# Attention output through folded weights, a hand-set order, and weight sums made early, in a linear-attention and token-mixer kernel

## The chip, the cores and the metric

One core of one Trainium2 chip. The metric is device time in microseconds (us), median over runs. A profiled execution has a span that is about 1.8 us shorter than the time of the same run; spans and moments within them come from the profile, medians from the timed runs. TensorE (PE) multiplies, VectorE (DVE) and ScalarE (ACT) do the elementwise work, SyncE (SP) issues nearly all DMAs, GpSimd (POOL) is nearly idle. PSUM is the memory in which matmuls add up their results. The granted clock is the share of TensorE's full clock that the chip let it have.

## The reference, cut to what matters

Batch 1, 2048 tokens, width 1024, 32 heads of 32, mixer width 3584, all bfloat16.

```python
pq, pk = phi(q), phi(k)                        # phi(t) = (t+1 if t>0 else exp(t)) + 1e-6
kv  = einsum("bhsd,bhse->bhde", pk, v)         # per head 32x32
z   = einsum("bhsd->bhd", pk)
num = einsum("bhqd,bhde->bhqe", pq, kv)
den = einsum("bhqd,bhd->bhq", pq, z)[..., None] + 1e-6
h   = x + (num / den).reshape(B, S, D) @ wo
# then a mixer over tokens: two layer norms of h, u = gelu(hn^T w1 + b1), y = u w2 + b2, h + y^T
```

## The kernel before: the parts that the change touches

The stages are: keys and values; the **Q phase** (query projection, with numerators and denominators of earlier tokens between its units); the **output projection** (16 tiles of 128 tokens, each "seeded": its residual tile is copied into PSUM, and the matmuls add to it); the **first mixer** (7 quads, each of two groups of 256 of the 3584 columns); the second mixer. The products of both mixers use 7 block products where plain ones need 8; a quad further does two of its seven products (p1 and p5) together, again by 7 in place of 8 ("inner").

```python
def attn_num_den(i):                       # per tile of 128 tokens
    for j in range(ND):                    # 8 matmuls, 128 numerator + 4 denominator columns
        nc.tensor.matmul(nd_ps[...], lhsT=pqT[:, j, i*P:(i+1)*P], rhs=ndrhs[:, j, :], start=True, stop=True)
    ... # ACT: ln, exp(-x) of 36 columns; DVE: 3 multiplies out of PSUM into o_sb
def attn_transpose(i, o_sb):
    nc.sync.dma_start_transpose(out=pqT[:, :, i*P:(i+1)*P], in_=o_sb[:])

def out_proj(i):
    xr = xrs.pop(i)                        # residual tile, loaded three tiles ahead
    h_bf = a3w.tile([P, D], BF16, name="h_bf")      # pool a3w: 3 buffers
    for dc in range(NDC):
        ap_ = acc_tile()                            # 5 PSUM banks in a ring
        nc.scalar.copy(ap_, xr[...])                # seed
        ... # 8 matmuls: pqT x wo
        nc.scalar.copy(h_bf[...], ap_)
        nc.vector.bn_stats(st[:, dc, :], ap_)
    ... # bn_aggr, scale, and:
    nc.sync.dma_start(h_dram[i][:], h_bf[:])
# ... after it: normalize_h(i - 2), which reads h_bf; at odd i also four differences ("combine")

# the first mixer's start: two products in a row, without the inner form
nxt = Mixer1(1)
pend = run_pair(cur, [], nxt)              # Mixer1(0)
cur, nxt = nxt, quad1(1)
pend = run_pair(cur, pend, nxt, after1=sums1, after5=sums5)
```

## Time and profile before

573.12 us median of 3 runs (573.01 to 573.24), span 571.5 us.

Part 4 of the page, the chain that ended last, by engine:

```profile
PE 95%; DVE 3%; ACT 1%; issue 1%; DMA 1%; ACTq 0%
```

The window sums by stage: the stretch, its length, then busy time (and instructions) of PE, PE's weight loads, DVE, ACT and POOL, the granted clock, DMA share and GB/s. The rows are the Q phase, the output projection, the first mixer, the rest.

```profile
core 0: us, PE busy (x) PEld busy (x) DVE busy (x) ACT busy (x) POOL busy (x), PEclk, DMA share, GB/s
125.92:178.14 52.22, 52.22 (x315) 26.68 (x313) 35.89 (x95) 34.69 (x79) 0.00 (x0) 1.00 0.66 167
178.14:235.50 57.36, 57.36 (x291) 26.73 (x289) 50.04 (x114) 40.12 (x100) 0.00 (x0) 1.00 0.56 149
235.50:403.03 167.53, 166.47 (x929) 90.64 (x929) 91.60 (x182) 79.34 (x163) 0.00 (x0) 1.00 0.25 76
403.03:571.50 168.47, 165.25 (x925) 89.87 (x923) 118.76 (x146) 34.14 (x73) 0.00 (x0) 1.00 0.47 127
```

PE is busy for the whole of the two attention stages; the others have slack. A busy PE may still run below its rate, so I read the rate from the starts of matmuls. PE's timeline in the Q phase (start, length, engine, line, operation, tiles, shape, count):

```profile
134.55 0.63 PE L1118 MATMUL nd_ps<-ndrhs,pqT 128*128 128x132 bf16 x8
135.02 3.61 PE L1019 MATMUL acc_t<-xnT,wq_sb 128*128 128x512 bf16 x16
138.47 0.63 PE L1118 MATMUL nd_ps<-ndrhs,pqT 128*128 128x132 bf16 x8
```

From 134.55 to 138.47 is 3.92 us. Sixteen matmuls of 512 columns take 138.47 - 135.02 = 3.45 us, 0.216 us each, and the 8 numerator ones 0.47 us. That is the exchange rate for the rest of the text. At the turn into the mixer PE does wait (the brackets give the idle time before a row and what ended it):

```profile
235.50 1.68 PE L297 MATMUL psA<-hE,wq 128*128 128x512 f16 x7
237.34 0.38 PE L297 MATMUL psA<-hE,wq 128*128 128x512 f16 x1 [0.15 <-DVE hE L1189]
237.55 1.67 PE L297 MATMUL psE<-hE,sa 128*128 128x512 f16 x7
239.96 1.02 PE L297 MATMUL psA<-hO,wq 128*128 128x512 f16 x4 [0.74 <-ACT psB L316]
```

### The profile page before, as it was taken

The page shows a single profiled execution, that of the slowest core. Times are in us where ns is not written, and L with a number is a line of the kernel's source. Part 1 is how long each engine was busy: PE and PEld are TensorE (multiplying, and loading weights), DVE is VectorE, ACT ScalarE, POOL GpSimd, SP SyncE. Part 2 cuts the span into 40 slices and gives each one's busy share as a digit, 9 for nine tenths or more (in the row PEclk, how much of TensorE's full clock was granted, in tenths as well). Part 3 has the DMA queues.
Part 4 walks back from the last instruction along what each step waited for, and adds up shares of the span by engine and source line. Part 5 has one row for each costly group of instructions (what it writes and reads, how often), then busy time and mean ns, then how long its engine had stood idle before and what let it go on. Part 6 is the DMA issues. An engine that isn't in the chain of part 4 may idle for free.

```text
span 571.5 us, 8308 instructions
## 1 busy us (share of the span) xinstructions
PE 563.7 (99%) x3124; PEld 293.3 (51%) x3124; DVE 390.2 (68%) x759; ACT 272.0 (48%) x585; POOL 1.8 (0%) x8
## 2 busy tenths in 40 slices
PE   7999999999999999999999999999999999999997
PEld 3444444455554444346555565555445655645643
DVE  6898887546767879873735627453979749659625
ACT  4747777666667776445445354453220411311211
POOL 1000000000000000000000000000000000000000
PEclk9999999999999999999999999999999999999999
DMA  9933432029536753104041340413892932912111
GB/s 303 357 76 79 89 74 38 19 96 323 118 72 127 177 178 111 55 2 147 1 148 28 120 148 1 148 48 81 205 255 84 244 96 75 278 56 73 38 47 46
DMA packets 97800, 66.61 MB, mean 117 GB/s; under 512 B 32082, under 2 KB 91744, under 8 KB 97760
## 3 DMA queue, kind: packets, MB, share of 16 engines
q1 hardware_dynamic: 97024, 65.42, 41.7%
q10 hardware_dynamic: 672, 0.66, 0.3%
q8 instruction: 24, 0.39, 0.3%
q14 instruction: 16, 0.13, 0.1%
q0 software_dynamic: 64, 0.01, 0.0%
HBM read 50.34 MB, written 8.39 MB: 103 GB/s over the span
## 4 chain that ended last, share of the span: by engine, by line
PE 95%; DVE 3%; ACT 1%; issue 1%; DMA 1%; ACTq 0%
PE psB L297 10%; PE psC L297 10%; PE acc_t L1019 9%; PE acc_t L1167 9%; PE psC L208 7%; PE psA L297 7%; PE psI L230 7%; PE psB L208 6%; PE psI L208 6%; PE psB L750 4%; PE psC L750 4%; PE psA L750 4%; PE psA L208 3%; PE acc_t L674 2%; PE psE L750 2%; PE psE L297 1%
## 5 line engine op out<-in xcount | busy, mean ns | idle before, releaser
L297 PEld LDWEIGHTS <-sa 128*128 128x128 f16 x436 | 42.6, 98 | 46.8 <-issue 0.7
L1019 PE MATMUL acc_t<-xnT,wq_sb 128*128 128x512 bf16 x256 | 58.0, 379 | 0.0
L1167 PE MATMUL acc_t<-wo_sb,pqT 128*128 128x512 bf16 x256 | 56.1, 379 | 0.0
L208 PEld LDWEIGHTS <-wq 128*128 128x128 bf16 (+1 forms) x357 | 34.5, 98 | 31.3
L297 PEld LDWEIGHTS <-wq 128*128 128x128 bf16 (+1 forms) x324 | 31.6, 98 | 33.1 <-issue 1.0
L208 PE MATMUL psC<-gs,wq 128*128 128x512 f16 (+2 forms) x210 | 45.0, 365 | 0.0
L1167 PEld LDWEIGHTS <-pqT 128*128 128x128 bf16 x256 | 24.8, 98 | 29.0
L1019 PEld LDWEIGHTS <-wq_sb 128*128 128x128 bf16 x256 | 24.5, 98 | 27.4
L166 ACT ACTIVATE e_sb<-acc_t 128x512 bf16<-128x512 f32 x40 | 23.9, 597 | 26.5 <-PE acc_t L1019 24.3
L170 DVE TENSOR_SCALAR e_sb<-e_sb 128x512 bf16<-128x512 bf16 x64 | 18.5, 289 | 25.4 <-ACT e_sb L166 24.8
L208 PEld LDWEIGHTS <-sa 128*128 128x128 f16 x231 | 22.6, 98 | 18.6
L750 PEld LDWEIGHTS <-xs 128*128 128x128 f16 x208 | 20.0, 98 | 23.3 <-DVE xs L736 1.3
L208 DVE TENSOR_TENSOR ot<-ot,hr 128x512 bf16<-128x512 bf16 (+2 forms) x27 | 11.2, 415 | 28.1 <-ACT ot L406 27.7
L333 ACT COPY psC<-psB 128x512 f32<-128x512 f32 x22 | 12.5, 570 | 35.1 <-PE psB L297 21.5
L297 PE MATMUL psB<-hT,sa 128*128 128x512 f16 x112 | 28.4, 379 | 0.0
L441 DVE TENSOR_TENSOR e<-psI,es 128x256 f32<-128x256 f32 x12 | 5.1, 425 | 34.0 <-PE psI L230 34.0
L297 PE MATMUL psC<-hT,wq 128*128 128x512 f16 x112 | 28.3, 379 | 0.0
L750 PE MATMUL psA<-wkv,xnT 128*128 128x512 bf16 x104 | 26.7, 379 | 0.0
L1178 DVE BATCH_NORM_STATS2 hst<-acc_t 128x6 f32<-128x512 f32 x32 | 22.1, 692 | 6.7 <-ACT h_bf L1177 6.5
L297 PE MATMUL psA<-hO,wq 128*128 128x512 f16 x112 | 25.6, 379 | 0.7 <-ACT psB L316 0.7
L297 PE MATMUL psB<-hO,sa 128*128 128x512 f16 x112 | 25.5, 379 | 0.0
L297 PE MATMUL psC<-hT,sa 128*128 128x512 f16 x112 | 25.5, 379 | 0.0
(184 smaller groups left out, 1022.9 us busy)
## 6 DMA issues: line engine op xcount, KB each, us to landing
wq<-in_B_w_dram SPq DMA_DIRECT2D x14, 1024.0 KB, 7.7
wq<-in_B_w_dram SPq DMA_DIRECT2D x8, 1792.0 KB, 9.1
xr<-in_A_x_dram SPq DMA_DIRECT2D x16, 256.0 KB, 3.1
h_dram<-h_bf SPq DMA_DIRECT2D x16, 256.0 KB, 2.2
hr<-h_dram SPq DMA_DIRECT2D x32, 128.0 KB, 2.4
out_dram<-ot SPq DMA_DIRECT2D x31, 128.0 KB, 1.8
x_sb<-in_A_x_dram SPq DMA_DIRECT2D x15, 256.0 KB, 3.2
wkv<-in_A_wqkv_dram SPq DMA_DIRECT2D x2, 1024.0 KB, 9.0
```

The costliest lines, as they stand in the source:

```text
L166: pin(nc.scalar.activation(e_sb[:], src, ACT.Exp))
L170: pin(nc.vector.tensor_scalar(e_sb[:], e_sb[:], 1.0, PHI_EPS, ALU.min, ALU.add))
L208: return (lambda *a, **kw: pin(op(*a, **kw))) if Held.on else op
L230: pe.matmul(ps, lhsT=self.lhs[m][:, k, :], rhs=self.mov[m][:, k, :], start=(start and k == 0), stop=(k == self.nk - 1), skip_group_check=True,
L297: pe.matmul(ps[:, cols], lhsT=lhs[:, k, :], rhs=mv(k)[:, cols], start=(start and k == 0), stop=(k == self.nk - 1), skip_group_check=True,)
L333: nc.scalar.copy(self.C[:], self.B[:])
L441: dve.tensor_tensor(self.sts[m].e[:, self.cols(h)], ps, es, ALU.add)
L674: mm = nc.tensor.matmul(pp[:, 0:CW], lhsT=xnT[:, kt, i * P:(i + 1) * P], rhs=wkv[:, kt, c * CW:(c + 1) * CW], start=(kt == 0), stop=(kt == ...
L750: pin(nc.tensor.matmul(ps[:], lhsT=lhs[:, k, :], rhs=rhs[:, k, :], start=(start and k == 0), stop=(k == hk2 - 1), skip_group_check=True,))
L1019: nc.tensor.matmul(qp[:, 0:SW], lhsT=wq_sb[:, kt, j * P:(j + 1) * P], rhs=xnT[:, kt, u * SW:(u + 1) * SW], start=(kt == 0), stop=(kt == ND ...
L1167: nc.tensor.matmul(ap_[:, 0:CW], lhsT=pqT[:, j, i * P:(i + 1) * P], rhs=wo_sb[:, j, dc * CW:(dc + 1) * CW], start=(j == 0 and not SEED_RES ...
L1178: nc.vector.bn_stats(st[:, dc, :], ap_[:, 0:CW])
```

## The change: intent and diff

- **Fold.** num @ wo is pq @ (kv @ wo), so the block-diagonal kv is multiplied into wo once (8 transposes, 16 matmuls), and queries go straight into the output projection. The division moves to the queries: denominators of 512 tokens come from 8 matmuls in four 32-column tiles of the array, their inverses go to HBM and return broadcast over the 32 rows of a head, and DVE multiplies the queries by them. 128 numerator matmuls, 48 multiplies out of PSUM and 16 transposing DMAs go.
- **First quad.** Mixer groups 0 and 1 run as one quad, with p5 as an inner product; its weight sums are made in the Q phase; two direct products cover the last tile's differences.
- **Order and loads.** The attention stages and the first mixer are held in written order (`ht`, `hs`, `hv`, `hd` pin each instruction of PE, ACT, DVE, SP); residual tiles are loaded five tiles ahead.

```diff
+            def fold(j):
+                for c in range(NDC):
+                    ht.matmul(ps[:, 0:CW], lhsT=kvT[:, j, :], rhs=wo_sb[:, j, cols], start=True, stop=True)
+                    (hs.copy if c == 0 else hv.tensor_copy)(wf[:, j, cols], ps[:, 0:CW])
+            def den_mm(u):                      # [cut: loops o in 2, g in 4; j = 4 * o + g]
+                        ht.matmul(ps[g * QR:(g + 1) * QR, :], lhsT=zz[:, j, ...], rhs=pqT[:, j, u * SW:(u + 1) * SW],
+                                  start=(o == 0), stop=(o == 1), tile_position=(0, g * QR))
+            def den_inv(u, ps):
+                hs.activation(ps[:], ps[:], ACT.Ln, bias=eps_den[:], scale=1.0 / S)
+                hs.activation(rd[:], ps[:], ACT.Exp, scale=-1.0)
+                hd.dma_start(rd_dram[u][:], rd[:])
+                for h in range(2):              # [cut: rdb, 3 buffers]
+                    for q in range(HB):         # 8 broadcast reads of 128 KB in all
+                        hd.dma_start(rdb[q * DH:(q + 1) * DH, :, :], rows[h, q].unsqueeze(0).to_broadcast([DH, 4, SW]))
+            def scale_q(u, h):
+                hv.tensor_tensor(v, v, rdbs.pop((u, h))[:], ALU.mult)
-            for i in range(NS):                 # [cut]
-                if i + XRL < NS: load_xr(i + XRL)
-                out_proj(i)
+            scale_at = {0: (NSC - 2, 1), 4: (NSC - 1, 0), 5: (NSC - 1, 1)}
+            for i in range(NS):
+                seed(i + 1)
+                load_xr(i + XRL + 2)
+                out_mm(i)
+                if i == 0:
+                    den(NSC - 1)
+                if i == NS - 1:
+                    h_scale(i - 1)
+                    normalize_h(i - 2)
+                    normalize_h(i - 1)
+                out_evac(i)                     # h_bf (still 3 buffers), bn_stats, h_dram write
+                if 0 < i < NS - 1: h_scale(i - 1)
+                if i in scale_at: scale_q(*scale_at[i])
+                if 2 <= i < NS - 1: normalize_h(i - 2)
-    pend = run_pair(cur, [], nxt)
-    pend = run_pair(cur, pend, nxt, after1=sums1, after5=sums5)
+    Held.on = True
+    sums5()
+    pend, nxt = cur.run_first(quad1(1), sums1)
```

## The prediction

> **What bounds it now.** TensorE. In the chain of work that ended last PE holds 95%; the window sums show PE busy 52.20 of 52.20 us in the Q phase (125.9 to 178.1) and 57.40 of 57.40 in the output projection (178.1 to 235.5), with DVE at 35.87 and 50.08, ACT at 34.67 and 40.16. The chain's merged pieces give 1.73 us for 8 matmuls of 512 columns (0.216 each); the timeline shows the Q phase repeating 16 such and 8 numerator matmuls every 3.92 us, so 8 of those 132-column ones cost 0.47 us. PE's loss in the middle lies mostly at the turn into the mixer: the timeline there shows holes of 0.15 us (for hE) and 0.74 us (for the copy psA to psB), and matmul starts spaced too far apart add up to about 2.2 us between 235.5 and 271.5, against 0.3 us in a steady quad of 23.6 us.
>
> **What the change does to PE.**
> - Removed: 128 numerator/denominator matmuls, 16 x 0.47 = 7.5 us.
> - Removed: the first mixer quad's shared product takes the 7-product form; 1024 columns fewer, 0.4 us.
> - Added: 8 transposes, 0.45 us; 16 fold matmuls of 512 columns, 3.45 us.
> - Added: 4 denominator groups, each 8 matmuls of 512 columns in four 32-column tiles. The Trainium skill (TensorEngine Tiling, Key Properties) says that such tiles run in parallel and that changing the mode drains the array; no trace here shows either yet. If four overlap: two rounds of 0.22 us plus fill and two drains, which I estimate at 1.0 us a group from the matmul's 379 ns against its 216 ns cadence: 4.0 us. If not: 8 x 0.216 plus drains, about 2.1 us a group, 8.5 us.
> - Turn into the mixer: two products of the quad (6.9 us) run before anything needs the last token tile's differences, and weight sums are done in the Q phase. I expect 1.9 of the 2.2 us back.
>
> Sum: -7.5 -0.4 -1.9 +0.45 +3.45 +4.0 = -1.9 us, so 571.2; without overlap +2.6 us, 575.7.
>
> **Off PE: nearly nothing to the time.** DVE loses 48 multiplies out of PSUM (16.4 + 6.6 us) and gets 8 copies (about 0.6 each) and 8 multiplies of 128x2048 (about 1.2 each, from today's 2048-wide sums). Sixteen transposing DMAs (3.1 us each) become 4 writes and 32 broadcast reads through HBM; at least six units of 1.73 us pass between a denominator and the first multiply by it, which should cover about 6 us of DMA. Both engines keep slack in each stage. Loading the residual further ahead buys nothing: no wait of PE for it is in the table of waits.
>
> **Predicted:** 571.2 us, 568.8 to 575.5 (8 in 10). Faster by over 2%: 0.02; within 2%: 0.95; slower by over 2%: 0.03.
>
> **What would show it.** The Q phase takes the sum above with PE still about 100% busy; consecutive denominator matmuls start a few ns apart in fours (overlap) or 216 ns apart (none); the output projection falls to 256 x 0.216 = 55.3 us plus one group; the losses at the turn shrink to under 0.5 us; steady quads stay at 23.6 us and the second mixer is the same.
>
> **What would make it wrong.** No overlap of column tiles, or costlier drains. The pinned order: an early fold waiting for its weights (two 1 MB loads), a multiply waiting for the broadcast, or one late DVE or ACT instruction that holds PE because nothing may pass it. Mixer quads changed by the new place of the last product's evacuation: 0.3 us a quad either way is 2 us.

## The result, and the profile after

574.84 us median of 4 runs (574.75 to 576.84) against 573.14 of before: ratio 1.0038, 95% interval 1.0016 to 1.0060. Ratios here are the mean time of one kernel's runs over that of the other's in the same rounds, so not quite the ratio of the medians quoted. Run again later with the experiments it gave 575.53 (575.33 to 576.31) against 573.33, ratio 1.0041 (1.0027 to 1.0055). So it is a little slower: the predicted range holds it, the predicted 571.2 doesn't, and the sign was wrong. That the range holds it is luck: it reached up to 575.5 for column tiles that don't overlap (575.7 by the sum), and they did overlap; what filled the range was a loss that the prediction had put at nearly nothing.

The same four window rows of the changed kernel:

```profile
125.89:178.46 52.57, 52.31 (x262) 23.23 (x265) 35.43 (x84) 37.30 (x70) 0.00 (x0) 1.00 0.53 162
178.46:237.65 59.19, 56.54 (x265) 25.02 (x264) 44.47 (x91) 40.86 (x96) 0.00 (x0) 1.00 0.52 174
237.65:404.54 166.89, 165.92 (x942) 91.83 (x941) 93.94 (x188) 78.19 (x164) 0.00 (x0) 1.00 0.25 76
404.54:573.10 168.56, 165.24 (x925) 89.76 (x923) 119.59 (x147) 34.13 (x73) 0.00 (x0) 1.00 0.47 127
```

Against before: Q phase +0.35 us, output projection +1.83, first mixer -0.64, the rest +0.09; together +1.6, the difference of the spans. The stage that lost its 4 numerator groups is the one that got longer, and DVE and ACT are still far from full in it. PE's timeline, first a denominator group in the Q phase and the transposes, then the output projection:

```profile
134.61 0.62 PE L208 MATMUL den_ps<-pqT,zz 128*32 128x512 bf16 x8
135.16 1.90 PE L208 MATMUL acc_t<-xnT,wq_sb 128*128 128x512 bf16 x8
136.90 0.61 PE L208 MATMUL acc_t<-ident,kvbd 128*128 128x128 bf16 x8
137.56 3.40 PE L208 MATMUL acc_t<-xnT,wq_sb 128*128 128x512 bf16 x15
```

```profile
182.55 13.99 PE L208 MATMUL acc_t<-wo_sb,pqT 128*128 128x512 f16 x64
198.25 7.07 PE L208 MATMUL acc_t<-wo_sb,pqT 128*128 128x512 f16 x32 [1.71 <-ACT acc_t L208]
205.87 3.61 PE L208 MATMUL acc_t<-wo_sb,pqT 128*128 128x512 f16 x16 [0.55 <-ACT acc_t L208]
209.79 28.03 PE L208 MATMUL acc_t<-wo_sb,pqT 128*128 128x512 f16 x128 [0.30 <-ACT acc_t L208]
```

A group of 8 denominator matmuls takes 0.55 us start to start, less than the 1.0 I allowed: within it they start at 0, 4, 7, 10 and 227, 230, 234, 237 ns, two rounds of four that overlap. That agrees with the Trainium skill (TensorEngine Tiling, Key Properties), that different tiles can execute in parallel. But the output projection has holes at tiles 5, 7 and 8, each ended by ACT writing a seed.

Who held ACT? The waits of the stage (178 to 216 us), each with its sum, count and longest:

```profile
DVE hst L208 <- ACT h_bf L208: 10.3, 5, 5.2
ACT h_bf L208 <- DMA h_dram<-h_bf: 4.5, 1, 4.5
ACT h_bf L208 <- DVE hE L208: 2.7, 2, 2.0
PE acc_t L208 <- ACT acc_t L208: 2.6, 3, 1.7
```

ACT's copy of a finished tile into h_bf waits 4.5 us for a DMA, the write of an earlier h tile to HBM. (The tile's own matmuls end at about 193, so the DMA accounts for some 3.2 us of it.) ACT's timeline around it:

```profile
190.59 1.09 ACT L208 CAST acc_t<-xr 128x512 f32<-128x512 bf16 x2
196.22 1.07 ACT L208 CAST h_bf<-acc_t 128x512 bf16<-128x512 f32 x2 [4.53 <-DMA h_dram<-h_bf]
197.62 1.09 ACT L208 CAST acc_t<-xr 128x512 f32<-128x512 bf16 x2
```

And the DMA issues of SP in the same stretch:

```profile
184.07 0.33 SPq L208 DMA_DIRECT2D rd_dram<-rd  x1
188.17 3.65 SPq L208 DMA_DIRECT2D rdb<-rd_dram  x8
191.94 0.36 SPq L208 DMA_DIRECT2D h_dram<-h_bf  x1
192.40 0.38 SPq L208 DMA_DIRECT2D xr<-in_A_x_dram  x1
192.87 0.39 SPq L208 DMA_DIRECT2D h_dram<-h_bf  x1
```

The inverse denominators are written at 184.07. The reads may start when that write has landed, 4.1 us later, and SP waits for it (from the waits of SP, 178 to 216 us):

```profile
SPq L208 <- DMA rd_dram<-rd: 3.7, 1, 3.7
```

After that the 8 issues take 3.65 us. The h write of tile 0, whose data were ready at 185.0, stands behind them and is issued at 191.94. So my **theory A**: the queue is held for 7.9 us by DMAs that nothing urgent needs; h writes land late; the three h buffers stay taken; ACT can't empty tile 3; DVE's statistics of it follow ACT's copy; the PSUM banks stay full; the next seeds, and PE, wait. **Rival B**: DVE has too much to do in a fixed order (three multiplies of 128x2048, 1.22 us each, went into this stage). **Rival C**: the residual tiles come late, behind the same reads.

### The profile page after: what moved, and what is told of

It reads as the page before. It is cut to its first block, busy times and chain, and to the rows that moved or that the text cites. A ratio compares the mean times of both kernels' runs of the same rounds, so it can differ in the third digit from the quotient of the medians.

```text
span 573.1 us, 8144 instructions
## 1 busy us (share of the span) xinstructions
PE 562.5 (98%) x3049; PEld 289.7 (51%) x3064; DVE 387.7 (68%) x734; ACT 274.3 (48%) x573; POOL 1.8 (0%) x8
## 4 chain that ended last, share of the span: by engine, by line
PE 86%; DVE 8%; ACT 3%; DMA 2%; issue 1%; SPq 0%; ACTq 0%; DVEq 0%
PE psC L208 15%; PE psB L208 15%; PE psI L208 13%; PE acc_t L208 9%; PE psA L208 7%; PE psB L796 4%; PE psC L796 4%; PE psA L796 4%; DVE hst L208 3%; PE acc_t L720 2%; PE psB L298 2%; PE psA L298 2%; PE acc_t L1065 2%; PE psE L796 2%; PE psC L298 2%; DVE hT L208 1%
## 5 line engine op out<-in xcount | busy, mean ns | idle before, releaser
L208 PEld LDWEIGHTS <-wq 128*128 128x128 bf16 (+1 forms) x653 | 63.4, 98 | 55.7 <-issue 1.2
L208 PEld LDWEIGHTS <-sa 128*128 128x128 f16 x651 | 63.6, 98 | 54.8
L208 PE MATMUL acc_t<-wo_sb,pqT 128*128 128x512 f16 x256 | 56.2, 379 | 2.6 <-ACT acc_t L208 2.6
L208 PEld LDWEIGHTS <-is 128*128 128x128 f16 x376 | 36.7, 98 | 18.4 <-issue 3.6
L208 PE MATMUL acc_t<-xnT,wq_sb 128*128 128x512 bf16 x188 | 43.1, 379 | 0.2
L208 PEld LDWEIGHTS <-wq_sb 128*128 128x128 bf16 x192 | 18.5, 98 | 23.0 <-issue 1.3
L208 DVE TENSOR_TENSOR e<-psI,es 128x256 f32<-128x256 f32 x20 | 8.5, 423 | 31.9 <-ACT es L254 19.3
L208 DVE BATCH_NORM_STATS2 hst<-acc_t 128x6 f32<-128x512 f32 x32 | 20.8, 688 | 12.5 <-ACT h_bf L208 12.4
L208 DVE TENSOR_TENSOR psA<-psI,es 128x256 f32<-128x256 f32 x18 | 7.8, 432 | 27.0 <-PE psI L208 24.4
L241 ACT COPY psI<-psI 128x256 f32<-128x256 f32 x19 | 6.9, 361 | 38.1 <-PE psI L208 38.1
```

The lines of the kernel that those rows point to most:

```text
L208: return (lambda *a, **kw: pin(op(*a, **kw))) if self.always or Held.on else op
L241: nc.scalar.copy(self.b, self.a)
```

## The experiments

Each edits the changed kernel unless said otherwise. The medians of before in the four batches were 573.32, 573.21, 573.33 and 573.28 us.

### Twice as many h buffers

```diff
-a3w = a3.enter_context(tc.tile_pool(name="a3w", bufs=3))
+a3w = a3.enter_context(tc.tile_pool(name="a3w", bufs=6))
```

> Edit: the pool of h tiles of the output projection has 6 buffers in place of 3. Theory A: the 3.3 us that TensorE loses at 198 to 214 us come from the one DMA queue: the last denominators' write and 8 broadcast reads hold it from 184.1 to 191.9 us, the h writes behind them land late, the h tiles stay occupied, ScalarE cannot copy tile 4 out, and the PSUM banks are not given back. With 6 buffers ScalarE need not wait: the projection falls from 59.2 us to about 56, the run by about 3 us against the changed kernel, to about 571.8. Rival B (VectorE has too much to do in a fixed order, because of the three 128x2048 multiplies): only the first hole (1.88 us) goes, those at tiles 7 to 9 (1.4 us) stay, about 573. Rival C (the residual tiles come late behind the same reads): the first hole stays, about 574.5.

Measured: 571.97 us (571.62 to 572.52), ratio to before 0.9979 (0.9962 to 0.9995). The whole projection runs without a hole, 240 matmuls in a row:

```profile
182.08 0.62 PE L208 MATMUL den_ps<-pqT,zz 128*32 128x512 bf16 x8
182.63 51.97 PE L208 MATMUL acc_t<-wo_sb,pqT 128*128 128x512 f16 x240
```

The stage takes 55.91 us in place of 59.19 (178.53 to 234.44), 3.3 us less. SP still issues the first h write at 191.80: the queue is as late as before, but no one waits for it.

```profile
191.80 0.36 SPq L208 DMA_DIRECT2D h_dram<-h_bf  x1
```

A holds; B and C, which left holes, don't.

### The denominators' DMAs on another queue

```diff
-                hd.dma_start(rd_dram[u][:], rd[:])
+                hg.dma_start(rd_dram[u][:], rd[:])       # hg pins GpSimd; the 8 reads likewise
```

> Edit: the denominators' write and their broadcast reads are issued by GpSimd's queue instead of SyncE's; 3 h buffers. Theory A: the h writes are issued at once, all four holes go, about 3 us less than the changed kernel (571.8), unless that queue is slow and the multiplies at tiles 4 and 5 come late. Rival B: holes at tiles 7 to 9 stay (about 573). Rival C: as A for the first hole, since the residual loads are freed too, so this run does not tell A from C.

Measured: 572.63 us (572.47 to 574.42), ratio 0.9996 (0.9981 to 1.0011); the span is 570.2 us, the same as with 6 buffers, and the projection takes 55.90 us (178.48 to 234.38) with 3 buffers. The first h write is issued 6.9 us earlier than in the changed kernel, and PE runs without a hole:

```profile
185.05 0.33 SPq L208 DMA_DIRECT2D h_dram<-h_bf  x1
182.57 51.97 PE L208 MATMUL acc_t<-wo_sb,pqT 128*128 128x512 f16 x240
```

Taking the holder out of the queue does what buffering against it does. Time less span is 2.27 us here against 1.81 with 6 buffers, so about 0.5 us goes outside the span; why is open. The Trainium skill (DMA: Bandwidth & Descriptors, Issuing engines are not separate DMA queues) says that all issuing engines share the same 16 DMA engines and that using several saves only issue time, "which is usually small relative to the DMA itself". Here moving 9 DMAs to another issuer was worth 3.3 us of the stage, and not because the h writes landed faster (median 4.6 us here and 4.7 in the changed kernel, both from 184 to 197 us): SP no longer stood waiting for a landing while they were ready. The denominators' write itself landed in 2.0 us here and in 4.1 there; why isn't shown.

### Without the last two multiplies (wrong output on purpose)

```diff
-scale_at = {0: (NSC - 2, 1), 4: (NSC - 1, 0), 5: (NSC - 1, 1)}
+scale_at = {0: (NSC - 2, 1)}
```

> Edit: the two multiplies of the last 512 tokens by their inverse denominators are left out (wrong output on purpose for these tokens), the DMAs stay. Theory A: the first hole (1.88 us at tile 5) stays, the later ones shrink because VectorE catches up 2.5 us sooner: about 1 us less than the changed kernel. Rival B: all holes go, 3 us less. Rival C: the first hole stays.

Measured: 574.30 us (573.14 to 576.36); the output is wrong, as meant. In the profile the first hole stays and is even longer, the later ones are gone:

```profile
182.52 13.99 PE L208 MATMUL acc_t<-wo_sb,pqT 128*128 128x512 f16 x64
199.91 39.83 PE L208 MATMUL acc_t<-wo_sb,pqT 128*128 128x512 f16 x176 [3.40 <-ACT acc_t L208]
```

So B is refuted for the first hole. The later ones may be DVE catching up after it, with the multiplies in its way; but this profile doesn't separate that from its longer first hole, which also gave DVE more time. The time doesn't confirm my "1 us less": the median is 0.5 us below the changed kernel's, with runs spread over 3.2 us, probably since the first hole itself changes from run to run (below).

The long hole brought something that I hadn't expected. The first seven matmuls after it start 216 ns apart, the next eight 427. The window sums, cut where the clock's records change, show the granted clock (third number from the end):

```profile
197.81:201.22 3.41, 1.31 (x7) 0.60 (x7) 2.63 (x6) 3.17 (x8) 0.00 (x0) 1.00 0.70 270
201.22:204.63 3.41, 3.41 (x10) 1.21 (x9) 2.81 (x7) 2.26 (x6) 0.00 (x0) 0.50 0.59 164
204.63:208.04 3.41, 3.41 (x17) 1.55 (x16) 2.77 (x6) 2.74 (x7) 0.00 (x0) 1.00 0.45 146
```

The clock's own records have it at one half for 3.4 us. The Trainium skill (TensorE: Matmul & The Clock Gate, What's actually happening) puts the array at half its clock after an idle window of about 3.4 us. The runs agree in size: idle times of 1.71 us (the changed kernel) and 2.52 us (the same kernel run again) left the clock alone, and those of 3.40 us here and 4.62 us in the next experiment halved it. They don't agree in detail (idle times rest on the modelled ends of matmuls). Here the half clock begins 1.3 us after the hole has ended, and in the 3.41 us just before it PE was idle for only 2.10; in the next experiment it begins at 195.79, 3.0 us after PE went idle. So a full 3.4 us of idling was not needed. The time then pays twice, hole and slow matmuls (8 x 0.21 = 1.7 us here).

### Residual tiles three tiles ahead again

```diff
-            for i in range(XRL + 1):             # first loads
+            for i in range(XRL):
-                    load_xr(XRL + 1)             # in the Q phase, at seed(0)
-                load_xr(i + XRL + 2)
+                load_xr(i + XRL)
```

> Edit: the residual tiles are loaded three tiles ahead as in the kernel before, in place of five. Theory A: it changes nothing while the residual tiles are not what is late, within 0.5 us of the changed kernel, or a little worse because the loads behind the reads now gate the seeds at tile 3. Rival C (residual loads are the cause): clearly slower, by over 2 us.

Measured: 577.37 us (577.14 to 578.54), ratio 1.0076 (1.0061 to 1.0091). I expected no change, and was wrong by 2.5 us against the changed kernel's 574.84 (1.8 us against its later 575.53); by the line that I had drawn, over 2 us, the first figure speaks for C. Now ACT waits for the residual:

```profile
196.77 1.11 ACT L208 CAST acc_t<-xr 128x512 f32<-128x512 bf16 x2 [6.38 <-DMA xr<-in_A_x_dram]
```

PE's hole at 197.41 is 4.62 us, with a halved clock after it. So C names a real wait, but one that the change had already moved out of the way; what is behind it is the same held queue. Two runs test that.

> Edit: as e2_denpool (denominator DMAs on GpSimd's queue, 3 h buffers) with the residual tiles loaded three ahead again. Theory A (revised: one queue held by the denominators starves two things behind it, the residual loads if they are three ahead, else the h writes): with the queue free, three ahead is enough; within 0.5 us of e2_denpool (572.5), against 577.4 for three ahead on the held queue. Rival C (three ahead is too late in itself): 3 us or more above e2_denpool.

Three ahead *with the denominators' DMAs on GpSimd's queue*: 572.34 us (572.07 to 572.47), ratio 0.9981 (0.9965 to 0.9997). With the queue free, three ahead is enough.

> Edit: 6 h buffers as in e1_hbf6 and the residual tiles three ahead as in e4_xr3, the denominator DMAs on SyncE's queue. Theory A (two things stand behind the denominators' reads in one queue; each alone is enough to stop TensorE): the residual of tile 3 comes at about 196.8 us as in e4_xr3, the hole of 4 to 5 us at 193 to 197 us stays and with it the lower clock after it; 576 to 577.5, about 4.5 us over e1_hbf6 (571.97). So five ahead is worth about 4.5 us once the h buffers are out of the way. Rival (the h buffers alone were behind both holes): about 572.

Three ahead *with 6 h buffers and the queue held*: 577.45 us (576.26 to 578.86), ratio 1.0075 (1.0052 to 1.0098); the hole, which is at tile 4 in both profiles (tiles counted from 0), stays (3.9 us of waiting on the seed, which waits 5.7 us for the residual). So two things stood behind the denominators in one queue, and either alone was enough to stop PE. Five ahead is worth about 5.5 us once the h buffers are out of the way (577.45 - 571.97), of which some 1.7 us is the halved clock (3.4 us of it in this profile).

### Denominators without column tiles

On top of the 6 buffers, the stationary tile is padded to 128 columns, so that one matmul fills the array. The result is the same.

```diff
-  ht.matmul(ps[g*QR:(g+1)*QR, :], lhsT=zz[:, j, ...], ..., start=(o == 0), stop=(o == 1), tile_position=(0, g*QR))
+  ht.matmul(ps[:], lhsT=zw[:, j, :], ..., start=(j == 0), stop=(j == ND - 1))   # zw: zeros but for j's 4 columns and unused rows
```

> Edit: on top of e1_hbf6, the denominators' matmuls use a 128-column stationary tile padded with zeros, so one matmul fills the array and no column tiles are used; the result is the same. Theory P (four 32-column tiles overlap): a group takes 8 x 0.216 = 1.73 us in place of the 0.55 us seen, four groups 4.7 us more than e1_hbf6 (571.97), 576.7. Rival (the group's 0.55 us is an artefact of how the trace models ends, and the work is serial anyhow): within 0.5 us of e1_hbf6.

Measured: 575.73 us (575.55 to 577.47), ratio 1.0049 (1.0035 to 1.0063), 3.8 us over the version with column tiles. A group takes 1.73 us:

```profile
134.97 1.89 PE L208 MATMUL den_ps<-pqT,zw 128*128 128x512 bf16 x8
136.70 1.89 PE L208 MATMUL acc_t<-xnT,wq_sb 128*128 128x512 bf16 x8
```

1.73 against 0.55 is 3.1 times for four tiles. The two attention stages grew by 3.6 and 1.1 us, the 4.7 expected; the first mixer was 0.8 us shorter in this profile, in part since waits of 0.22 and 0.30 us that the 6-buffer profile has in later quads are absent. Without column tiles the change would not have paid even with the 6 buffers: 575.73 against 573.33 of before.

### The first mixer: part undone, order freed

Both on top of the 6 buffers. First, the first quad undone: no early sums, `run_pair` as before, and no holding in the mixer.

```diff
-    Held.on = True
-    sums5()
-    cur.mov5 = mov5
-    pend, nxt = cur.run_first(quad1(1), sums1)
+    nxt = Mixer1(1)
+    pend = run_pair(cur, [], nxt)
+    cur, nxt = nxt, quad1(1)
+    pend = run_pair(cur, pend, nxt, after1=sums1, after5=sums5)        # [cut: sums back at tile 10]
```

> Edit: on top of e1_hbf6, the mixer part of the change is undone: no weight sums in the Q phase, the first two products run as a pair without the shared inner product, as in the kernel before, and the first mixer's order is the scheduler's. My prediction gave this part 2.3 us (0.4 for columns, 1.9 for the turn), so 2.3 us longer than e1_hbf6, 574.3. The stage times of e1_hbf6 against the kernel before (167.2 against 167.5 us) say 0.3 to 0.8 us, about 572.5.

Measured: 574.28 us (574.03 to 575.32), 2.3 us over the 6 buffers. That equals my prediction for this part (the other forecast, 572.5 from the stage times, missed), but not by its reasons alone, since the run also takes the holding off: up to the second quad's p2 it is 1.2 us behind (270.21 against 269.04), and the rest is lost in later quads, whose code is the changed one and is now ordered by the scheduler. Second, only the holding off:

```diff
-    Held.on = True
     sums5()
```

> Edit: on top of e1_hbf6 (6 h buffers; 570.2 us span, mixer stage 167.2 us from its first matmul to the second mixer's first), the first mixer's instructions are left to the scheduler, not held in written order. Theory H (the held order costs the mixer about 1 us: holes of 0.2 to 0.5 us that vary with the quad): the quads come back to 23.57 us each, the stage gets about 1 us shorter. Rival T (the holes come from the way the stage is written, not from the hold): unchanged within 0.3 us. Rival G (the hold is what makes this order work): 1 us or more longer.

Measured: 574.01 us (573.87 to 574.75), 2.0 us longer: rival G. The mixer of the changed kernel needs its held order; its 1 us of small holes has another cause.

### Two repairs of the order, on top of the 6 buffers

At the turn PE waited 0.22 us for DVE and 0.39 us for ACT's copy psA to psB, which stood behind ACT's scale of tile 15, which waited for DVE's statistics, which stood behind four differences that nothing needed yet.

```diff
                 if i == NS - 1:
                     h_scale(i - 1)
-                    normalize_h(i - 2)
+                    normalize_h(i - 2, False)        # without the differences of tiles 12 and 13
                     normalize_h(i - 1)
                 out_evac(i)
             h_scale(NS - 1)
+            combine_pair(NS // 2 - 2)
             normalize_h(NS - 1)
```

> Edit: on top of e1_hbf6, at the last token tile VectorE does the statistics of tile 15 before, not after, the four differences of tiles 12 and 13. Theory: the two holes at the turn (0.26 us for hE of tile 14 and 0.56 us for the copy psA to psB, which waits on ScalarE behind the scale of tile 15, which waits for VectorE) shrink to under 0.2 us together; about 0.7 us less than e1_hbf6 (570.2 to 569.5 us of span). Rival (the wait only moves to the differences, which come later now, and to the inner product that reads them): a new hole of about the same size at the first inner product, no gain.

Measured: 570.99 us (570.74 to 572.86), ratio 0.9965 (0.9943 to 0.9987), 1.0 us less than the 6 buffers alone. The turn has no hole:

```profile
235.10 3.62 PE L208 MATMUL psA<-hE,wq 128*128 128x512 f16 x16
238.56 3.62 PE L208 MATMUL psA<-hO,wq 128*128 128x512 f16 x16
```

The profile of this kernel fell on its slowest run and has a hole of 0.93 us in a later quad, at 329.39. There DVE had waited 2.44 us for a 1 MB weight load before the next quad's sums (ended at 320.07), in fixed order, so this quad's adds, ACT's gelu after them and ACT's copy for the inner product came late. When the load lands varies (the same wait was 0.58 us in the 6-buffer profile), and with it the holes. The last version moves 1.3 us of those sums behind the adds:

```diff
                 st.p2()
-            pre(6)
             for st in self.sts:                     # [cut: before_p7()]
                 st.p7(...)
+            pre(6)
```

> Edit: f2_turn (6 h buffers, statistics of the last tile first) and, in each mixer quad, VectorE adds the two shared halves of this quad's products before, not after, the next quad's second weight sums, which wait for a 1 MB load. Theory: the holes before the second inner product of a quad (up to 1.09 us in f2_turn, varying with when the load lands) come from VectorE standing at that load in fixed order; 1.3 us of work less ahead of the adds removes them; 0.4 to 1.0 us less than f2_turn (570.99), about 570.3. Rival (the holes come from ScalarE's own order): no change.

Measured: 570.86 us (570.75 to 572.48), ratio 0.9964 (0.9950 to 0.9977). In its profile that hole is gone (the longest wait of PE left in the later quads is 0.30 us at 378.37, which the version without this step has too, at 380.36), and the first mixer takes 166.10 us:

```profile
178.51:234.41 55.90, 55.90 (x265) 25.08 (x264) 45.02 (x92) 40.65 (x96) 0.00 (x0) 1.00 0.55 185
234.41:400.51 166.10, 165.72 (x941) 91.85 (x940) 93.62 (x187) 78.88 (x164) 0.00 (x0) 1.00 0.25 77
```

But the median is only 0.13 us below the version without this last step, from other rounds, so the 0.4 to 1.0 us that I expected of it isn't shown. It beats before by 0.4% and the changed kernel by 0.8% (ratio of the two ratios, 0.9964 over 1.0041).

### The changed kernel again

> The changed kernel unedited, for a time of the same rounds: 574.8 +- 0.5 us by its earlier runs, one run in four 2 us longer with a granted clock of 0.996 or 0.997[...].

575.53 us; its first hole was 2.7 us in this profile (spacing of the matmuls less their columns' time) where the first profile had 1.9, and all later stages keep their lengths within 0.6 us. So the length of the hole, set by when DMAs land, makes most of the difference between the changed kernel's runs. That its one run of 576.84 us, at a granted clock of 0.996, had a hole long enough to halve the clock is likely but was not traced.

## Why the prediction was right or wrong

- **What bounds it: right.** PE does, and its columns and holes explain every stage.
- **Removed matmuls, fold, transposes: right in size.** The transposes took 0.66 us in place of 0.45.
- **Denominator group: mechanism right, size off in the safe direction.** I put 1.0 us; it is 0.55, plus 0.1 before it. Four groups are about 1.4 us cheaper than predicted. This is why the Q phase grew by 0.35 us where my sum gave -5.6 + 0.45 + 3.45 + 3.0 = +1.3.
- **The first quad and the turn: too high.** I expected 2.3 us. The stage got 0.64 us shorter, in part since 0.6 us of waiting stayed at the turn and small holes came in later quads; with the two repairs it is 1.43 us shorter (167.53 to 166.10).
- **"Off PE: nearly nothing to the time": this step failed.** I asked whether the broadcast would come in time for its *own* reader, and it did. I didn't ask what else stands behind it in the same queue. The output projection should have been 256 x 0.216 + 1.0 = 56.3 us; it was 59.2, and 55.9 once the h tiles had buffers.
- **"Loading the residual further ahead buys nothing": wrong.** The table of waits of before said nothing about a queue that the change would fill. In the changed kernel it saves 1.8 to 2.5 us, with 6 h buffers 5.5; only with the queue free does it buy nothing (572.63 with five ahead, 572.34 with three).
- **What would make it wrong** named the pinned order and a late instruction that holds PE. That is the family of the cause, but the h writes were not in the list.

So a time near the predicted 571.2 would have come about (571.97 with 6 buffers, 570.99 with the turn repaired too) had three h buffers not met a held queue. Even then the nearness is partly luck. With 6 buffers the two attention stages came out about 1.4 us better than my sum (+0.41 and -1.45 us against +1.3 and -0.9), and the first mixer 2.0 us worse (-0.34 against -2.3).

## What to carry to other kernels

When a change puts a DMA that must wait for another DMA into a queue, cost the queue for everyone: list what stands behind it, how long it is held (here 4.1 us of landing and 3.65 us of issuing), and how many buffers each of those streams has to live through it. Buffers are only counted as enough against the old latency; recount them, or give the waiting DMAs a queue of their own. And a stage where no engine is full can still lose time, so follow PE's hole back by the waits (seed, copy, buffer, DMA, queue) before blaming the busiest engine.

## What the Trainium skill lacked or had wrong

- DMA: Bandwidth & Descriptors, Issuing engines are not separate DMA queues: it counts only the sequencer's issue time as what several issuing engines save. It lacks the cost of an issuing engine's wait for a landing, which holds everything behind it: 7.9 us here, 3.3 us of a stage, gone when the 9 DMAs moved to another engine's queue.
- TensorE: Matmul & The Clock Gate, Measured speedup vs the span model: it has no figure for four column tiles at 512 columns. The runs show 0.55 us for a group of two such rounds against 1.73 us untiled, 3.1 times.
- TensorEngine Tiling, Key Properties: it says that changing the mode drains the array and gives no cost. A group's first matmul and the one after the group each started about 0.1 us later than their columns explain.
- TensorE: Matmul & The Clock Gate, What's actually happening: its table has the clock halved after at least one idle window of about 3.4 us. The runs show it halved after less: PE had been idle for 2.10 of the 3.41 us before 201.22 in the run without the last two multiplies, and for 3.0 us with three residual tiles ahead. It then stayed halved for 3.4 and 6.8 us.
- Runtime: NRT & Kernel Launch, The ~15µs preamble/postamble breakdown: among the times outside a kernel it has none for DMAs issued by GpSimd. They left the span at 570.2 us and added about 0.5 us to the run.
